# Batch 0 of a cosformer attention by halves of its heads, ahead of a two-GEMM MLP

## The chip, the cores and the metric

The kernel runs on one core of a Trainium2 chip. The metric is the device time of one execution in microseconds: 300.6 us is the median of three runs of the kernel before the change (300.25 to 301.1). The profile is of one further execution, whose span on the core is 298.9 us.

## The reference

A linear attention with position-weighted features, followed by an MLP with a squared ReLU. There are 8 batches, 8 heads, 576 positions and a head width of 64; the model width is 512 and the hidden width 2048.

```python
def phi(x, c, s):                        # c = cos, s = sin of pi/2 * pos / 576
    r = np.maximum(x, 0.0)
    return np.concatenate([r * c, r * s], axis=-1)
q_p, k_p = phi(q, cos_w, sin_w), phi(k, cos_w, sin_w)
kv  = np.einsum('bhsf,bhsd->bhfd', k_p, v)
z   = np.sum(k_p, axis=2)
num = np.einsum('bhsf,bhfd->bhsd', q_p, kv)
den = np.einsum('bhsf,bhf->bhs', q_p, z)[..., None] + 1e-06
x   = (num / den)                        # heads side by side: 4608 rows of 512
h   = np.maximum(x @ w_in, 0.0)          # w_in 512 x 2048
out = (h * h) @ w_out                    # w_out 2048 x 512
```

## The kernel before

Each batch is cut into four pieces of 128 positions (`j` = 0 to 3, "main") and a tail of 64 positions (`j` = 4 = `J`), whose two halves of the heads lie above each other on the partitions. The kernel's work is a list of "column slots": `gemm1` slots multiply x (transposed) by a part of w_in, `gemm2` slots multiply the squared hidden values by w_out. The attention of later batches is put between these slots. Batch 0's attention has no slots to lie between and stands ahead of them.

The loads of batch 0 go out on SyncE's queue, one issue for the main part of each of k, v, q, and two for each tail:

```python
    def load(src, nm, b, eng):
        main = inp.tile([P, H, J, D], F32, name=nm, tag=nm, bufs=2)
        tail = inp.tile([P, HH, D], F32, name=nm + "t", tag=nm + "t", bufs=2)
        eng.dma_start(out=main[:, :, :, :],
                      in_=src[b, :, 0:MAIN, :].rearrange("h (p j) d -> p h j d", j=J))
        for g in range(2):
            eng.dma_start(out=tail[g * TAIL : (g + 1) * TAIL, :, :],
                          in_=src[b, g * HH : (g + 1) * HH, MAIN:S, :].rearrange("h p d -> p h d"))
```

What stands ahead of the first slot, in the order in which each engine gets it:

```python
        load_batch(0, nc.sync, "kvq")
        constants()
        for j in range(NS):
            att_k(0, j)                  # cosine features on VectorE, sine features on ScalarE
            if j < J:
                warm(j)                  # two matmuls of 512 columns whose result nobody reads
        att_v(0, J - 1, nc.gpsimd, H - 1, H)   # one head of v cast by GpSimd
        att_v(0, 0, nc.vector)
        att_v(0, 1, nc.scalar)
        att_v(0, 2, nc.vector)
        att_v(0, 3, nc.vector, 0, H - 1)
        att_v(0, J, nc.vector)
        for i in range(4):
            load_w1(i, 4)                # GpSimd's queue, behind its cast
        load_batch(1, nc.gpsimd, "qkv")
        for i in range(4):
            load_w2(i, 4)
        load_batch(2, nc.gpsimd, "qkv")
        att_kv(0, 0)                     # kv and z in one: v has a column of ones
        att_kv(0, 1)                     # ends with a copy of kv from PSUM (kvz) on ScalarE
        for j in range(J):
            warm(j)
        att_feat(0, 0)                   # features of q, pieces 0 and 1
        att_feat(0, 1)
        for j in range(2):
            att_qT_pe(0, j, True)        # transposes of 8 heads on TensorE
        for j in range(2):
            att_qT_copy(0, j, True)      # PSUM to SBUF, half on VectorE, half on ScalarE
            att_num(0, j, True)
        for j in range(2):
            att_div(0, j)                # den, reciprocal, product on VectorE: x
        att_feat(0, 2, "s")
        att_feat(0, 3, "s")
        for j in range(2):
            fill(4 - j)                  # matmuls whose result nobody reads
            att_x_pe(0, j, True)         # x transposed on TensorE, copied by ScalarE
        att_feat(0, 2, "c")
        att_feat(0, 3, "c")
        att_qT_pe(0, 2)
        att_qT_copy(0, 2, True)
        for s in range(len(slots)):
            run(s)
```

`load_w1(i, 4)` and `load_w2(i, 4)` each bring a quarter of a weight matrix, converted from fp32 to bf16 by the DMA. `gemm1` slot `s` of a batch needs quarter `s % 4` of w1. Slots 0 to 7 are `gemm1` of batch 0; slots 8 to 15 are `gemm2` of batch 0, and slot 8 needs the first quarter of w2:

```python
        step = P if (b, s) == (0, 0) else w        # slot 0 in two parts of 128 columns
        for c in range(0, w, step):
            for i in range(nh):
                hb = h0 + i
                for kb in range(KB):
                    ...                            # matmul of w1sb[:, kb, hb] with xT[:, kb, c:c+step]
```

The two remaining pieces of batch 0 are finished between the first slots:

```python
    at(0, att_qT_pe, 0, 3)
    at(0, att_num, 0, 2)
    at(0, att_qT_copy, 0, 3, True)
    at(0, att_div, 0, 2)
    at(1, att_x_pe, 0, 2, True)
    at(1, att_d, 0, 3)
    at(2, att_x_pe, 0, 3, True)
```

Of the kernel before, what the change touches and what calls it, by code (L numbers as in the profile page):

```python
# [15 lines left out]
FP = 512  # L16
# [3 lines left out]
def kernel(  # L20
# [40 lines left out]
    def load(src, nm, b, eng):  # L61
        main = inp.tile([P, H, J, D], F32, name=nm, tag=nm, bufs=2)
        tail = inp.tile([P, HH, D], F32, name=nm + "t", tag=nm + "t", bufs=2)
        eng.dma_start(
            out=main[:, :, :, :],
            in_=src[b, :, 0:MAIN, :].rearrange("h (p j) d -> p h j d", j=J),
        )
        for g in range(2):
            eng.dma_start(  # L69
                out=tail[g * TAIL : (g + 1) * TAIL, :, :],  # L70
                in_=src[b, g * HH : (g + 1) * HH, MAIN:S, :].rearrange("h p d -> p h d"),
            )
        kqv[nm, b] = (main, tail)

    def load_batch(b, eng, order):
        for nm in order:
            load({"k": k, "v": v, "q": q}[nm], nm, b, eng)
# [6 lines left out]
    ident = const.tile([P, P], BF16, name="ident")  # L84
    cos_col = const.tile([P, J + 1], F32, name="cos_col")
    sin_col = const.tile([P, J + 1], F32, name="sin_col")

    def constants():
        sidx = const.tile([P, J + 1], F32, name="sidx")
        for p0, p1, c, n, base, mult in [  # L90
            (0, P, 0, J, 0, J),
            (0, TAIL, J, 1, MAIN, 1),
            (TAIL, P, J, 1, MAIN, 1),
        ]:
            nc.gpsimd.iota(
                sidx[p0:p1, c : c + n],
                pattern=[[1, n]],
                base=base,
                channel_multiplier=mult,
                allow_small_or_imprecise_dtypes=True,  # L100
            )
        bias_pi2 = const.tile([P, 1], F32, name="bias_pi2")
        nc.vector.memset(bias_pi2, math.pi / 2.0)
        theta_scale = (math.pi / 2.0) / S
        nc.scalar.activation(cos_col, sidx, ACTF.Sin, bias=bias_pi2[:], scale=-theta_scale)
        nc.scalar.activation(sin_col, sidx, ACTF.Sin, bias=0.0, scale=theta_scale)
        make_identity(nc, ident)

# [52 lines left out]
    def xT_of(b, i):  # L161
        return cached(xts, (b, i), [P, KB, 2 * P], "xT", 4)
# [5 lines left out]
    def feat_cos(dst, src, j):  # L168
        nc.vector.tensor_scalar(  # L169
            out=dst[:, :, 0:D],  # L170
            in0=src,
            scalar1=0.0,
            scalar2=cos_col[:, j : j + 1],
            op0=ALU.max,
            op1=ALU.mult,
        )

    def feat_sin(dst, src, j):
        nc.scalar.activation(  # L179
            out=dst[:, :, D:F], in_=src, func=ACTF.Relu, scale=sin_col[:, j : j + 1]  # L180
        )

    def att_k(b, j):
        for f in (feat_cos, feat_sin):
            f(kp_of(b, j), piece("k", b, j), j)

    def att_v(b, j, eng, h0=0, h1=H):
        copy = eng.copy if eng is nc.scalar else eng.tensor_copy
        vx, vxt = vexts[b % 2]
        if j == J:  # L190
            copy(out=vxt[:, :, 0:D], in_=piece("v", b, j))
        else:
            copy(out=vx[:, j, h0:h1, 0:D], in_=piece("v", b, j)[:, h0:h1, :])  # L193

    def warm(j):

        wm = ps_h.tile([P, 2, FP], F32, name="wm", tag="hps", bufs=2)
        for i in range(2):
            nc.tensor.matmul(  # L199
                out=wm[:, i, :],  # L200
                lhsT=ident[:, :],
                rhs=kp_of(0, j)[:, i * HH : (i + 1) * HH, :],
                start=True,
                stop=True,
            )

    def fill(n):

        wm = ps_a.tile([P, 2, FP], F32, name="wm", tag="pa", bufs=1)
        for i in range(n):  # L210
            nc.tensor.matmul(  # L211
                out=wm[:, i % 2, :],
                lhsT=ident[:, :],
                rhs=kp_of(0, 0)[:, 0:HH, :],
                start=True,
                stop=True,
            )

    def att_kv(b, part):
        vx, vxt = vexts[b % 2]  # L220
        if part == 0:
            kvzs[b] = att.tile([P, H, E1], BF16, name="kvz", tag="kvz", bufs=2)
            kzs[b] = ps_a.tile([P, 2, FP], F32, name="kz", tag="pa", bufs=1)
        kz = kzs[b]
# [4 lines left out]
        for j in (0, 1) if part == 0 else range(2, NS):  # L229
            for hh in range(HH):  # L230
                for half in range(2):
# [12 lines left out]
                    )  # L244
        if part == 1:
            nc.scalar.copy(
                out=kvzs[b].rearrange("p (a h) e -> p a (h e)", a=2),
                in_=kz[:, :, 0 : HH * E1],
            )

    def att_feat(b, j, parts="cs"):
        for c in parts:
            f = feat_cos if c == "c" else feat_sin
            f(qp_of(b, j), piece("q", b, j), j)
# [15 lines left out]
    def att_qT_pe(b, j, apart=False):  # L270

        nh = H if j < J else HH
        tq = ps_y.tile([P, H, P], BF16, name="tq", tag="yps", bufs=2)
        tqs[b, j] = [tq[:, 0:HH, :]]
        if apart:
            hi = ps_h.tile([P, HH, P], BF16, name="tqh", tag="hps", bufs=2)
            tqs[b, j].append(hi)
        elif nh == H:
            tqs[b, j].append(tq[:, HH:H, :])
        for h in range(nh):  # L280
            nc.tensor.transpose(  # L281
                tqs[b, j][h // HH][:, h % HH, :], qp_of(b, j)[:, h, :], ident[:, :]
            )

    def att_qT_copy(b, j, both=False):
        qpTs[b, j] = []
        for i, tq in enumerate(tqs[b, j]):
            t = att.tile([P, HH, P], BF16, name=f"qpTp{i}", tag=f"qpTp{i}", bufs=5)
            copy = nc.scalar.copy if both and i else nc.vector.tensor_copy
            copy(out=t[:, :, :], in_=tq[:, :, :])  # L290
            qpTs[b, j].append(t)

    def att_num(b, j, early=False):
        qpT, kvz = qpTs[b, j], kvzs[b]
        if early:
            num = ps_h.tile([P, 2, FP], F32, name="num", tag="hps", bufs=2)
        else:
            num = ps_a.tile([P, 2, FP], F32, name="num", tag="pa", bufs=1)
        for hh in range(HH):
            for half in range(2):  # L300
# [9 lines left out]
        nums[b, j] = num  # L310

    def att_div(b, j):
        n = 2 if j < J else 1
        n4 = nums[b, j][:, 0:n, 0 : HH * E1].rearrange("p b (h e) -> p b h e", e=E1)
# [7 lines left out]
            out=x_of(b, j).rearrange("p (b k) (l d) -> p b k l d", b=n, l=2),  # L322
# [18 lines left out]
    def att_x_pe(b, j, in_y=False):  # L341
        nk = KB if j < J else 2
# [4 lines left out]
        for kb in range(nk):  # L347
            nc.tensor.transpose(tx[:, kb, :], x_of(b, j)[:, kb, :], ident[:, :])  # L348
        if j < J:
            dst = xT_of(b, j // 2)[:, :, j % 2 * P : (j % 2 + 1) * P]  # L350
        else:
            dst = xT_tails(b // 2)[:, b % 2].rearrange("p k g c -> p k (g c)")
        nc.scalar.copy(out=dst, in_=tx[:, 0:nk, :])
# [5 lines left out]
    def gemm1(b, s):  # L359
# [9 lines left out]
        step = P if (b, s) == (0, 0) else w  # L369
# [125 lines left out]


    at(0, att_qT_pe, 0, 3)
    at(0, att_num, 0, 2)
    at(0, att_qT_copy, 0, 3, True)
    at(0, att_div, 0, 2)  # L500
    at(1, att_x_pe, 0, 2, True)
    at(1, att_d, 0, 3)
    at(2, att_x_pe, 0, 3, True)
# [48 lines left out]
    with tc.manual_schedule():  # L552
        load_batch(0, nc.sync, "kvq")
        constants()
        for j in range(NS):
            att_k(0, j)
            if j < J:
                warm(j)
        att_v(0, J - 1, nc.gpsimd, H - 1, H)
        att_v(0, 0, nc.vector)  # L560
        att_v(0, 1, nc.scalar)
        att_v(0, 2, nc.vector)
        att_v(0, 3, nc.vector, 0, H - 1)
        att_v(0, J, nc.vector)
        for i in range(4):
            load_w1(i, 4)
        load_batch(1, nc.gpsimd, "qkv")
        for i in range(4):
            load_w2(i, 4)
        load_batch(2, nc.gpsimd, "qkv")  # L570
        att_kv(0, 0)
        att_kv(0, 1)
        for j in range(J):
            warm(j)
        att_feat(0, 0)
        att_feat(0, 1)
        for j in range(2):
            att_qT_pe(0, j, True)
        for j in range(2):
            att_qT_copy(0, j, True)  # L580
            att_num(0, j, True)
        for j in range(2):
            att_div(0, j)
        att_feat(0, 2, "s")
        att_feat(0, 3, "s")
        for j in range(2):
            fill(4 - j)
            att_x_pe(0, j, True)
        att_feat(0, 2, "c")
        att_feat(0, 3, "c")  # L590
        att_qT_pe(0, 2)
        att_qT_copy(0, 2, True)
# [31 lines left out]
```

## Time and profile before

| | before |
|---|---|
| time, median of 3 runs | 300.6 us |
| span of the profiled execution | 298.9 us |
| TensorE matmul busy | 285.7 us (96%) |
| ScalarE busy | 154.0 us (52%) |
| VectorE busy | 135.5 us (45%) |
| GpSimd busy | 48.0 us (16%) |
| moved by DMA | 52.98 MB, mean 177 GB/s |

In the lines of the profile, PE is TensorE's matmuls, PEld its weight loads, DVE VectorE, ACT ScalarE, POOL GpSimd, SP SyncE. L380 is line 380 of the kernel. `out<-in` names the tiles that an instruction writes and reads, and a group in the timeline gives its start in us from the span's start and its length, with the idle time before it and what ended that in square brackets. Transposes on TensorE count as matmuls. A "landing" is the moment at which a DMA's completion reaches the semaphore that others wait on. GB/s counts the bytes written, so w1 and w2, which are read as fp32 and written as bf16, show half of what they read. In a table by stages, each row has the stage, its length, busy time and count of PE, PEld, DVE, ACT and POOL, the granted clock, the DMA share and GB/s.

### The profile page before, as it was taken

To read this page: it belongs to the slowest core of one execution; us is meant where nothing else is said; L and a number is where in the kernel's file an instruction comes from. 1 tells how busy PE (TensorE), PEld (TensorE's weight loads), DVE (VectorE), ACT (ScalarE), POOL (GpSimd) and SP (SyncE) were. 2 spreads that over 40 slices of the span, in tenths; PEclk is the share of its full clock that TensorE was granted. 3 is DMA by queue.
4 is the path that set the end of the run, shared out by engine and by line. 5 is a ranking of instruction groups with operands and counts; after the bars stand their busy time and mean duration, and the time that the engine had idled before them with its cause. 6 is when DMAs were issued, how large, how long until landed. Compare 5 with 4: busy or idle time off the path is not lost.

```text
span 298.9 us, 6372 instructions
## 1 busy us (share of the span) xinstructions
PE 285.7 (96%) x2636; PEld 200.6 (67%) x2659; DVE 135.5 (45%) x330; ACT 154.0 (52%) x215; POOL 48.0 (16%) x79
## 2 busy tenths in 40 slices
PE   0899999999999999999999999999999999999995
PEld 0469855889556984589654884589754894589544
DVE  1455664465648386228730287227740273024100
ACT  3466753666838564655554555555563552255311
POOL 1554304751121002000021001100021000100000
PEclk9999999999999999999999999999999999999999
DMA  7999993999648996896779925798669013100021
GB/s 216 293 206 352 276 243 102 352 362 209 171 99 148 242 269 157 239 278 181 122 170 221 334 47 124 235 271 227 114 178 212 35 37 79 72 36 2 33 75 70
DMA packets 77069, 52.98 MB, mean 177 GB/s; under 512 B 52240, under 2 KB 71952, under 8 KB 77040
## 3 DMA queue, kind: packets, MB, share of 16 engines
q1 hardware_dynamic: 67120, 29.50, 42.7%
q0 software_dynamic: 9776, 22.94, 26.8%
q8 instruction: 21, 0.34, 0.4%
q10 hardware_dynamic: 144, 0.13, 0.1%
q14 instruction: 8, 0.07, 0.1%
HBM read 36.70 MB, written 9.44 MB: 154 GB/s over the span
## 4 chain that ended last, share of the span: by engine, by line
PE 93%; DMA 3%; ACT 1%; issue 1%; DVE 1%; SPq 1%; ACTq 0%
PE hps L380 42%; PE yps L415 39%; PE kz L238 4%; PE num L307 3%; DMA v<-in_v_dram 3%; PE yh L415 2%; PE tq L281 1%; PE wm L199 1%; PE tx L348 1%; PE wm L211 1%; SPq L69 0%; ACT qpTp L290 0%; ACT rt L388 0%; DVE qpTp L290 0%; DVE gTt L395 0%
## 5 line engine op out<-in xcount | busy, mean ns | idle before, releaser
L380 PEld LDWEIGHTS <-w1sb 128*128 128x128 bf16 x1296 | 113.0, 98 | 12.3
L380 PE MATMUL hps<-xT,w1sb 128*128 128x256 bf16 (+1 forms) x1040 | 117.8, 271 | 0.0
L415 PE MATMUL yps<-w2sb,gT 128*128 128x512 bf16 (+1 forms) x476 | 108.1, 372 | 1.4 <-DVE qpTp L290 0.2
L388 ACT ACTIVATE rt<-hps 128x1024 bf16<-128x1024 f32 x72 | 73.7, 1024 | 57.8 <-DVE gT L395 32.6
L415 PEld LDWEIGHTS <-gT 128*128 128x128 bf16 x528 | 49.5, 98 | 53.0 <-DVE qpTp L290 0.7
L395 DVE TENSOR_TENSOR gT<-rt 128x1024 bf16<-128x1024 bf16 x64 | 44.0, 688 | 84.5 <-ACT rt L388 84.5
L411 POOL DMA_DIRECT2D out_dram<-ysb x34 | 20.7, 610 | 176.5 <-ACT ysb L401 174.3
L401 ACT COPY ysb<-yps 128x512 f32<-128x512 f32 (+1 forms) x35 | 20.0, 575 | 56.1 <-PE yps L415 56.0
L179 ACT ACTIVATE qp<-q,sin_col 128x512 bf16<-128x512 f32 x32 | 21.9, 718 | 5.0 <-DMA q<-in_q_dram 5.0
L179 ACT ACTIVATE kp<-k,sin_col 128x512 bf16<-128x512 f32 x32 | 21.1, 713 | 3.2 <-DMA k<-in_k_dram 3.2
L321 DVE TENSOR_TENSOR x<-num,rden 128x512 bf16<-128x512 f32 x32 | 22.1, 691 | 1.1
L169 DVE TENSOR_SCALAR qp<-q,cos_col 128x512 bf16<-128x512 f32 x32 | 14.4, 489 | 11.7 <-DMA q<-in_q_dram 11.7
L169 DVE TENSOR_SCALAR kp<-k,cos_col 128x512 bf16<-128x512 f32 x32 | 15.1, 481 | 5.0 <-DMA k<-in_k_dram 5.0
L317 DVE TENSOR_SCALAR den<-num 128x8 f32<-128x8 f32 (+1 forms) x40 | 6.6, 165 | 22.3 <-PE num L307 22.1
L380 PE MATMUL hps<-xTt,w1sb 128*128 128x128 bf16 x256 | 15.3, 219 | 0.0
L415 PE MATMUL yps<-w2sb,gTt 128*128 128x512 bf16 x64 | 14.5, 379 | 0.0
L193 DVE CAST vext<-v 128x512 bf16<-128x512 f32 (+1 forms) x31 | 13.0, 425 | 2.7 <-DMA v<-in_v_dram 2.7
L238 PEld LDWEIGHTS <-kp 128*128 128x128 bf16 x256 | 10.3, 102 | 4.0 <-issue 1.6
L199 PE MATMUL wm<-kp,ident 128*128 128x512 bf16 x15 | 6.0, 553 | 7.2 <-ACT kp L179 7.0
L307 PEld LDWEIGHTS <-qpT 128*128 128x128 bf16 (+1 forms) x240 | 10.3, 100 | 3.3 <-issue 1.7
L307 PE MATMUL num<-kvz,qpT 128*128 128x65 bf16 (+1 forms) x240 | 11.7, 194 | 0.0
L238 PE MATMUL kz<-vext,kp 128*128 128x65 bf16 x256 | 10.7, 199 | 0.8 <-DVE vext L193 0.8
(56 smaller groups left out, 130.2 us busy)
## 6 DMA issues: line engine op xcount, KB each, us to landing
out_dram<-ysb POOLq DMA_DIRECT2D x28, 256.0 KB, 3.5
k<-in_k_dram SPq DMA_DIRECT2D x5, 1024.0 KB, 6.1
v<-in_v_dram SPq DMA_DIRECT2D x5, 1024.0 KB, 8.1
q<-in_q_dram SPq DMA_DIRECT2D x5, 1024.0 KB, 6.0
q<-in_q_dram POOLq DMA_DIRECT2D x3, 1024.0 KB, 13.5
k<-in_k_dram POOLq DMA_DIRECT2D x3, 1024.0 KB, 10.3
v<-in_v_dram POOLq DMA_DIRECT2D x3, 1024.0 KB, 9.8
w1sb<-in_moe_w_in_dram POOLq DMA_DIRECT2D x4, 512.0 KB, 8.2
```

The source lines that it names most:

```text
L169: nc.vector.tensor_scalar(out=dst[:, :, 0:D], in0=src, scalar1=0.0, scalar2=cos_col[:, j : j + 1], op0=ALU.max, op1=ALU.mult,)
L179: nc.scalar.activation(out=dst[:, :, D:F], in_=src, func=ACTF.Relu, scale=sin_col[:, j : j + 1])
L193: copy(out=vx[:, j, h0:h1, 0:D], in_=piece("v", b, j)[:, h0:h1, :])
L238: nc.tensor.matmul(out=kz[:, half, hh * E1 : (hh + 1) * E1], lhsT=lhsT, rhs=rhs, start=(j == 0 and hh == 0), stop=(j == J and hh == HH - 1),)
L307: nc.tensor.matmul(out=out, lhsT=lhsT, rhs=kvz[:, half * HH + hh, :], start=True, stop=True)
L321: nc.vector.tensor_tensor(out=x_of(b, j).rearrange("p (b k) (l d) -> p b k l d", b=n, l=2), in0=n4[:, :, :, 0:D].rearrange("p b (k l) d -> ...
L380: nc.tensor.matmul(out=out, lhsT=w1sb[:, kb, hb * P : (hb + 1) * P], rhs=rhs, start=(kb == 0), stop=(kb == KB - 1),)
L388: nc.scalar.activation(out=rt[:, :, :], in_=hps[:, :, :], func=ACTF.Relu)
L395: nc.vector.tensor_tensor(out=dst, in0=rt[:, :, :], in1=rt[:, :, :], op=ALU.mult)
L401: nc.scalar.copy(out=ysb[:, c0:c1], in_=acc)
L411: eng.dma_start(out=dst, in_=ysb[p0 : p0 + n, c0:c1])
L415: nc.tensor.matmul(out=acc, lhsT=lhsT, rhs=w2sb[:, hb, c0:c1], start=(hb == 0), stop=(hb == HB - 1))
```

## The change

Batch 0 is loaded by halves of its heads: k, v, q of heads 0 to 3, then k, v, q of heads 4 to 7. Features, kv, num and x of the first half are worked through while the second half is on its way, so that after the last bytes only half of the heads is left to do. The first and the fifth column slot run in two parts of 128 columns, so that the first part can begin when the first piece of x is there. The warm-up matmuls read a tile of zeros and start at once instead of waiting for k. Query pieces 2 and 3 are transposed after slot 0. GpSimd still casts one head of v ahead of the weight loads; it is head 7, part of the second half.

The diff, cut to its core (helpers that only gained a `half` argument are left out, as marked):

```diff
-    def load(src, nm, b, eng):
-        main = inp.tile([P, H, J, D], F32, name=nm, tag=nm, bufs=2)
-        tail = inp.tile([P, HH, D], F32, name=nm + "t", tag=nm + "t", bufs=2)
+    def load(src, nm, b, eng, half=None):
+        ...                              # the two tiles, made once
+        main, tail = kqv[nm, b]
+        h0, h1 = (0, H) if half is None else (half * HH, (half + 1) * HH)
         eng.dma_start(
-            out=main[:, :, :, :],
-            in_=src[b, :, 0:MAIN, :].rearrange("h (p j) d -> p h j d", j=J),
-        )
-        for g in range(2):
+            out=main[:, h0:h1, :, :],
+            in_=src[b, h0:h1, 0:MAIN, :].rearrange("h (p j) d -> p h j d", j=J),
+        )
+        for g in range(2) if half is None else (half,):
 ... (features, v casts, kv, transposes, num, division, x: each for one half of the heads)
-    def warm(j):
+    def warm(n):
         wm = ps_h.tile([P, 2, FP], F32, name="wm", tag="hps", bufs=2)
-        for i in range(2):
+        for i in range(n):
             nc.tensor.matmul(
-                out=wm[:, i, :],
-                lhsT=ident[:, :],
-                rhs=kp_of(0, j)[:, i * HH : (i + 1) * HH, :],
-                start=True,
-                stop=True,
+                out=wm[:, i % 2, :], lhsT=ident[:, :], rhs=zeros[:, :], start=True, stop=True
             )
 ...
-        step = P if (b, s) == (0, 0) else w
+        step = P if b == 0 and s % 4 == 0 else w
 ...
-    at(0, att_qT_pe, 0, 3)
-    at(0, att_num, 0, 2)
-    at(0, att_qT_copy, 0, 3, True)
-    at(0, att_div, 0, 2)
-    at(1, att_x_pe, 0, 2, True)
-    at(1, att_d, 0, 3)
-    at(2, att_x_pe, 0, 3, True)
+    both = [nc.vector, nc.scalar]
+    for j in (2, 3):
+        at(0, att_qT_pe, 0, j)
+        at(0, att_qT_copy, 0, j, both)
+    at(1, att_d, 0, 2)
+    at(2, att_x_pe, 0, 2, True)
+    at(2, att_d, 0, 3)
+    at(3, att_x_pe, 0, 3, True)
 ...
-        load_batch(0, nc.sync, "kvq")
+        for half in range(2):
+            load_batch(0, nc.sync, "kvq", half)
         constants()
-        (the rest of the order ahead of slot 0, shown above)
+        warm(14)
+        for half in range(2):
+            for j in range(NS):
+                att_k(0, j, half)
+            if half == 1:
+                for j in range(2):
+                    fill(3)
+                    att_x_pe(0, j, True, 0)
+
+                att_v(0, 3, nc.gpsimd, None, (H - 1, H))
+                for i in range(4):
+                    load_w1(i, 4)
+                load_batch(1, nc.gpsimd, "qkv")
+                for i in range(4):
+                    load_w2(i, 4)
+                load_batch(2, nc.gpsimd, "qkv")
+            att_v(0, 0, nc.vector, half)
+            att_v(0, 1, nc.scalar, half)
+            att_v(0, 2, nc.vector, half)
+            if half == 0:
+                att_v(0, 3, nc.scalar, half)
+            else:
+                att_v(0, 3, nc.vector, None, (HH, H - 1))
+            att_v(0, J, nc.vector, half)
+            kv_mms(0, range(NS), (half,))
+            fill(4)
+            att_feat(0, 0, "cs", half)
+            att_feat(0, 1, "c", half)
+            kvz_copy(0, half, half + 1)
+            att_feat(0, 1, "s", half)
+            for j in range(2):
+                att_qT_pe(0, j, half)
+                att_qT_copy(0, j, [both[j]] * 2, half)
+            fill(2)
+            for j in range(2):
+                att_num(0, j, True, (half,))
+            for j in range(2):
+                att_div(0, j, half, half + 1)
+        att_feat(0, 2, "s")
         for j in range(2):
+            if j == 0:
+                fill(3)
+            att_x_pe(0, j, True, 1)
+        att_feat(0, 3, "s")
         att_feat(0, 2, "c")
         att_feat(0, 3, "c")
-        att_qT_pe(0, 2)
-        att_qT_copy(0, 2, True)
         for s in range(len(slots)):
             run(s)
```

## The prediction

> **What bounds the kernel now.** I read the page first: the span, the busy shares, the chain that ended last.
>
> ```profile
> span 298.9 us, 6372 instructions
> PE 285.7 (96%) x2636; PEld 200.6 (67%) x2659; DVE 135.5 (45%) x330; ACT 154.0 (52%) x215; POOL 48.0 (16%) x79
> ...
> PE hps L380 42%; PE yps L415 39%; PE kz L238 4%; PE num L307 3%; DMA v<-in_v_dram 3%; PE yh L415 2%; PE tq L281 1%; PE wm L199 1%; PE tx L348 1%; PE wm L211 1%; SPq L69 0%; ACT qpTp L290 0%; ACT rt L388 0%; DVE qpTp L290 0%; DVE gTt L395 0%
> ```
>
> TensorE holds 93% of the chain. Only a front part, before the first column slot, isn't a row of GEMM matmuls. So I next read the chain in order of time for the first 40 us (start, length, what).
>
> ```profile
> 2.71 8.13 DMA v<-in_v_dram
> ...
> 16.66 1.08 ACT qpTp L290 x2
> ...
> 21.05 1.79 PE hps L380 x32
> ...
> 37.49 0.46 PE tq L281 x8
> 37.95 0.02 issue
> 37.97 0.77 DVE qpTp L290 x2
> 38.74 0.05 issue
> 38.78 0.39 PE yps L415
> ```
>
> The first 10.8 us are loads of k and v, then batch 0's attention runs as one serial chain, and the first column slot begins at 20.9 (its first matmul; the chain books the end of the transposes to 21.05). From there the chain is TensorE without a gap, except for one small stop at 38. Seen like this, whatever pulls slot 0 forward shortens the whole kernel. Before believing that I asked what else the slots need: the weights. The timeline of GpSimd shows when their loads are issued.
>
> ```profile
> 10.89 0.49 POOL L193 CAST vext<-v 128x64 bf16<-128x64 f32 x1 [9.02 <-DMA v<-in_v_dram]
> 11.32 3.17 POOL L115 DMA_DIRECT2D w1sb<-in_moe_w_in_dram  x4
> ...
> 28.22 0.62 POOL L69 DMA_DIRECT2D vt<-in_v_dram  x1 [2.29 <-DMA q<-in_q_dram]
> 28.83 1.52 POOL L122 DMA_DIRECT2D w2sb<-in_moe_w_out_dram  x2
> ```
>
> GpSimd casts one head of v only after v has landed, and issues w1 behind it in its own order. After that its queue carries w1, batch 1, w2, batch 2. The DMA view cut to the first w1 issue, and cut to the first w2 issue, gives the time to landing (last column).
>
> ```profile
> w1sb<-in_moe_w_in_dram POOLq DMA_DIRECT2D x1, 512.0 KB, 5.5
> ...
> w2sb<-in_moe_w_out_dram POOLq DMA_DIRECT2D x1, 512.0 KB, 8.9
> ```
>
> So w1's first quarter is there at 11.32 + 5.5 = 16.8, 4.1 us before slot 0 uses it. The fourth is issued at 13.73 and takes 11.3, so it lands at 25.0; slot 3 starts at about 27.5, a slack of 2.5. And w2's first quarter lands at 28.83 + 8.9 = 37.7. Who uses it is in the timeline:
>
> ```profile
> 37.33 0.61 PE L281 MATMUL tq<-ident,qp 128*128 128x128 bf16 x8
> ...
> 37.80 0.39 PE L415 MATMUL yh<-w2sb,gT 128*128 128x512 bf16 x1
> ```
>
> Slot 8, the first of the second GEMM, starts at 37.80, and the weights it needs landed at 37.7. The slack is under 0.1 us. This is the number on which my prediction rests: the first 37.8 us have two limits of the same length, the TensorE chain and the DMA stream up to w2's first quarter. The chain shows only the first.
>
> **Is that stream full?** The DMA share is at or above 1 in nearly every stage from 5 to 35 us, with one hole, around the end of q:
>
> ```profile
> 12.40:12.80 0.40, 0.40 (x12) 0.40 (x10) 0.00 (x0) 0.00 (x0) 0.40 (x1) 1.00 0.72 197
> 12.80:13.20 0.40, 0.40 (x11) 0.31 (x9) 0.00 (x0) 0.00 (x0) 0.40 (x2) 1.00 0.53 101
> 13.20:13.60 0.40, 0.40 (x10) 0.31 (x10) 0.00 (x0) 0.00 (x0) 0.40 (x1) 1.00 0.60 98
> ```
>
> The last two columns are DMA share and GB/s. SyncE's loads run dry at about 13.2; the w1 stream, issued from 11.32, is at its full 205 GB/s of written bf16 only from about 14. From there to w2's landing it never pauses.
>
> **What the Trainium skill says.** "DMA: Bandwidth & Descriptors", section "Issuing engines are not separate DMA queues": DMAs started by different engines run on the same 16 DMA engines and interleave. The trace agrees: SyncE's queue has a 108% share alone from 11 to 12 us, GpSimd's 123% from 14 to 15, and between them they share. The same page, section "Anatomy of one DMA — SWDGE (gpsimd) path", gives a DMA from GpSimd a fixed 2.0 us or so besides its bytes. Here the first quarter of w1 takes 5.5, and successive quarters land about 2.7 apart, which leaves 2.8 fixed; I use the trace. "TensorE: Matmul & The Clock Gate", section "What's actually happening": a cold TensorE runs at half clock until about 3.4 us of activity, and an idle window of that length makes it cold again. The trace agrees with the warm-up: the 512-column warm matmuls start 0.43 apart at 7 us and 0.22 apart from 15.1 on.
>
> **The change part by part.**
> First, loads by halves. Bytes and packet sizes stay; twelve issues replace nine at 0.5 to 0.7 us each, so issuing still runs ahead of the bytes. In the new order (k, v, q of heads 0-3, then k, v, q of heads 4-7) the items end at sixths of the same 3.54 MB. In the kernel before k was there at 6.1 (0.73 + 5.4), v at 10.84 and q at 13.9. By bytes on that curve, k of the first half lands at about 4.7, v 6.3, q 8.7; of the second half k 10.5, v 12.5, q 14.1. So first-half data is far earlier, the last of q no earlier, and the **last of v comes 1.7 us later**, since half of q now lies ahead of it.
>
> Second, the path from the last q to slot 0. Half-width features: the 256-element tails took 0.35 on VectorE and 0.49 on ScalarE, against 0.48 and 0.71 at 512. From q at 14.1: sine features 0.5, transposes and their latency 0.4, copy 0.4 (ScalarE's for the second piece ends about 1 us later, behind the copy of kvz and its feature), num 0.3; then two divisions one after the other of about 0.85 (0.17 + 0.20 + some 0.45 for half of the 0.69), a transpose 0.4. That puts slot 0 at 18.3 to 18.5, against 20.89: **2.5 us gained** on this path.
>
> Third, work moved behind slot 0. The transposes of query piece 2 (0.6) leave the path before slot 0 and come after it, and slot 4 in two parts costs 32 matmuls in 1.95 instead of 16 in 1.75, so 0.2. Of the 2.5 some 1.7 would remain at slot 5.
>
> Fourth, GpSimd's cast now takes head 7, which comes with the second half. Its release moves from 10.84 to about 12.5, and with it the first w1 issue from 11.32 to 12.8 or 13.0. SyncE's loads still end at about 13.2, so the hole in the DMA stream grows by the whole delay; nothing makes it up, as the stream was full behind it. I take 1.5 us. Then w1 lands at 18.3, ..., 26.5, and w2's first quarter at 37.73 + 1.5 = 39.2.
>
> **The sum.** TensorE: slot 0 at 18.4, slot 3 held by w1 until 26.5 and done by 28.5 (29.5 before), slot 4 with 0.4 of added work, so ready for slot 8 at about 37.2. It must wait there until 39.2 or 39.3: 1.5 later than 37.80. Given back is the stop in slot 8 (third matmul at 38.24, next at 38.78 instead of 38.46: 0.3), as the copies it waited for are done during the wait. Net +1.2 us; everything after slot 8 is the same TensorE row and just moves. 300.6 + 1.2 = 301.8; I say 301.7.
>
> **Rivals.** (a) The gain survives: if w1 isn't late, 1.7 us come off at slot 5, but w2 still lands at 37.7, so slot 8 can't start earlier. Only the 0.3 of the stop would be won: 300.3. A real gain of 1.5 to 2 needs w2 earlier too, for which I see nothing in the diff: 299. (b) TensorE's idle stretch of about 2 us ahead of slot 8, or one between the halves at 11 to 13, makes it cold: cold slots 0 and 1 cost up to 3 us, most of it hidden by w2's lateness; a cold slot 8 costs 1.5 to 2: 303. The idle stretches are under the 3.4 us, so I give this a tenth. (c) v of the second half lands early, say at 11.7, because its small tails overlap: delay 0.8, time 301.1.
>
> **Range and chances.** The delay of w1 between 0.5 and 2.3 us gives 300.6 to 302.6; with (a) below and (b) above it I say 300.4 to 302.7. A change of 2% is 6 us, and no step here is worth that: same 0.98, the rest split.
>
> **What would show it.** Right: the first w1 issue at 12.5 to 13.2; slot 0's first matmul at 18 to 19; w2's first quarter landing at 38.8 to 39.7 and slot 8 starting with it after TensorE idled 1 to 2.5 us; from there the same spacing. Wrong: w1 issued at 11.5 or earlier, slot 8 starting before 37.5, or TensorE late for slot 8 by itself, with w2 waiting.

## The result, and the profile after

The changed kernel takes 302.84 us (median of 4 runs, 302.63 to 303.92) against 300.65 us for the kernel before on the same chip. The ratio is 1.008, with a 95% interval of 1.0052 to 1.0107: 2.2 us slower. The prediction was 301.7 with a range up to 302.7, so the direction was right and the size was half of what came. The profile is of the slowest of the four executions (303.92); the other three took 302.63 to 302.86, so the distances read from it below are about 1 us longer than in a typical one.

The page of the changed kernel, span, busy shares and the granted clock in tenths:

```profile
span 302.1 us, 6482 instructions
PE 290.9 (96%) x2687; PEld 203.5 (67%) x2687; DVE 139.0 (46%) x347; ACT 156.4 (52%) x227; POOL 47.4 (16%) x79
...
PEclk9969999999999999999999999999999999999999
```

Look at the third digit of the clock row: in the slice from 15.1 to 22.7 us TensorE had 0.6 of its speed on average. All 9s stood in that row before. The second thing to see is what is not there: from the fifth column slot on the activation of every slot of the first GEMM starts 2.96 us later in the changed kernel, to within 0.01 us, up to the last. So 2.96 of the 3.2 us between the two spans arise up to slot 4, and behind it the same work just moves, as the prediction said. The rest, 0.3 us, lies at the very end: from the landing of the last output to the end of the execution the changed kernel and each of its variants below take 1.22 to 1.23 us in their profiles, the kernel before and its variants 0.92 to 0.93. No part of the prediction has it, and its cause is open.

The table of stages of the changed kernel has the granted clock third from the right:

```profile
14.00:16.00 2.00, 0.53 (x12) 0.43 (x12) 1.94 (x6) 1.53 (x5) 2.00 (x4) 1.00 0.49 38
...
18.00:20.00 2.00, 1.55 (x13) 1.00 (x11) 0.42 (x1) 1.30 (x4) 2.00 (x4) 0.50 1.24 203
20.00:22.00 2.00, 1.62 (x13) 0.97 (x14) 1.83 (x8) 0.97 (x2) 0.55 (x2) 0.50 1.24 209
```

TensorE hardly works from 14 to 16 us (0.53), VectorE is full there (1.94), and from 16.8 to 23.7 the clock is at half. The DMA share from 14 to 16 is 0.49: the predicted hole, grown. Now the chain in order of time (start, length, what):

```profile
3.35 6.30 DMA q<-in_q_dram
...
13.27 1.28 DVE kp L192 x4
...
15.12 0.91 DVE vext L220 x3
...
16.06 0.53 DVE vextt L220
...
16.92 0.97 PE kz L234 x4
...
21.66 0.39 PE tx L377 x2
22.06 2.62 PE hps L409 x32
...
33.11 2.80 PE hps L409 x32
```

The chain no longer comes from the last loads. It comes from the *first* half's q, runs through the first half's divisions, then through VectorE's k features and v casts of the second half (13.27 to 16.59), then a row of filling matmuls at half clock (0.97), and slot 0 itself takes 2.6 instead of the 1.8 that the same 32 matmuls had in the chain before. The second half of k had landed at 11.4 and waited for VectorE; v had landed at 13.1 and q at 14.5.

The weights. GpSimd's timeline, and the DMA view cut to the first w2 issue:

```profile
13.13 0.24 POOL L220 CAST vext<-v 128x64 bf16<-128x64 f32 x1 [11.25 <-DMA v<-in_v_dram]
13.30 3.16 POOL L122 DMA_DIRECT2D w1sb<-in_moe_w_in_dram  x4
...
31.30 1.52 POOL L129 DMA_DIRECT2D w2sb<-in_moe_w_out_dram  x2
```

```profile
w2sb<-in_moe_w_out_dram POOLq DMA_DIRECT2D x1, 512.0 KB, 8.4
```

w1's first issue went from 11.32 to 13.30, and w2's first quarter lands at 31.30 + 8.4 = 39.7 instead of 37.7. Last, slot 8:

```profile
40.28 0.61 PE L306 MATMUL tq<-ident,qp 128*128 128x128 bf16 x8
...
40.73 0.59 PE L444 MATMUL yh<-w2sb,gT 128*128 128x512 bf16 x2
```

Slot 8 starts right behind the transposes, 1 us after w2 landed. In this execution TensorE itself was late, not the weights. Two explanations of the loss stand: **stream** (w2's first quarter, at the end of a DMA stream that started late, holds slot 8) and **chain** (VectorE's order and the half clock make TensorE late by itself). The runs had to tell whether it was one, the other, or both.

### The profile page after: what moved, and what is told of

The parts are those of the page before. It is cut to its first block, busy times and chain, and to the rows that moved or that the text cites. A ratio compares the mean times of both kernels' runs of the same rounds, so it can differ in the third digit from the quotient of the medians.

```text
span 302.1 us, 6482 instructions
## 1 busy us (share of the span) xinstructions
PE 290.9 (96%) x2687; PEld 203.5 (67%) x2687; DVE 139.0 (46%) x347; ACT 156.4 (52%) x227; POOL 47.4 (16%) x79
## 3 DMA queue, kind: packets, MB, share of 16 engines
q1 hardware_dynamic: 67168, 29.50, 40.7%
## 4 chain that ended last, share of the span: by engine, by line
PE 92%; DVE 2%; DMA 2%; ACT 1%; SPq 1%; issue 1%; ACTq 0%
PE hps L409 42%; PE yps L444 39%; PE num L335 3%; PE kz L264 3%; PE yh L444 2%; DMA q<-in_q_dram 2%; PE tq L306 1%; PE tx L377 1%; DVE x L350 1%; PE kz L234 1%; SPq L75 0%; ACT qp L201 0%; DVE kp L192 0%; SPq L70 0%; PE tqh L306 0%
## 5 line engine op out<-in xcount | busy, mean ns | idle before, releaser
L409 PEld LDWEIGHTS <-w1sb 128*128 128x128 bf16 x1312 | 114.2, 98 | 12.7 <-issue 0.6
L409 PE MATMUL hps<-xT,w1sb 128*128 128x256 bf16 (+1 forms) x1056 | 119.0, 271 | 0.5 <-ACT xT L382 0.5
L444 PE MATMUL yps<-w2sb,gT 128*128 128x512 bf16 (+1 forms) x496 | 110.6, 372 | 0.2 <-DVE qpTp L316 0.2
L417 ACT ACTIVATE rt<-hps 128x1024 bf16<-128x1024 f32 x72 | 73.7, 1024 | 58.9 <-DVE gT L424 32.8
L440 POOL DMA_DIRECT2D out_dram<-ysb x34 | 20.5, 605 | 176.2 <-ACT ysb L430 174.2
L201 ACT ACTIVATE qp<-q,sin_col 128x512 bf16<-128x512 f32 (+1 forms) x34 | 22.7, 695 | 7.7 <-DMA q<-in_q_dram 7.7
L350 DVE TENSOR_TENSOR x<-num,rden 128x512 bf16<-128x512 f32 (+1 forms) x34 | 22.4, 660 | 1.2
L201 ACT ACTIVATE kp<-k,sin_col 128x512 bf16<-128x512 f32 (+1 forms) x36 | 22.0, 667 | 1.6 <-DMA k<-in_k_dram 1.6
L192 DVE TENSOR_SCALAR qp<-q,cos_col 128x512 bf16<-128x512 f32 (+1 forms) x34 | 14.9, 478 | 11.9 <-DMA q<-in_q_dram 11.8
L192 DVE TENSOR_SCALAR kp<-k,cos_col 128x512 bf16<-128x512 f32 (+1 forms) x36 | 16.0, 458 | 3.1 <-DMA k<-in_k_dram 3.1
L444 PE MATMUL yps<-w2sb,gTt 128*128 128x512 bf16 x64 | 14.5, 379 | 0.0
L220 DVE CAST vext<-v 128x512 bf16<-128x512 f32 (+2 forms) x33 | 13.3, 410 | 2.1 <-DMA v<-in_v_dram 2.1
L444 PEld LDWEIGHTS <-gTt 128*128 128x128 bf16 x64 | 6.3, 98 | 7.5
```

Source lines behind the costliest of these rows:

```text
L192: nc.vector.tensor_scalar(out=dst[:, :, 0:D], in0=src, scalar1=0.0, scalar2=col_of(cos_col, j, half), op0=ALU.max, op1=ALU.mult,)
L201: nc.scalar.activation(out=dst[:, :, D:F], in_=src, func=ACTF.Relu, scale=col_of(sin_col, j, half))
L220: copy(out=dst, in_=src)
L350: nc.vector.tensor_tensor(out=x_of(b, j)[:, 2 * b0 : 2 * b1].rearrange("p (b k) (l d) -> p b k l d", b=n, l=2), in0=n4[:, :, :, 0:D].rearr ...
L409: nc.tensor.matmul(out=out, lhsT=w1sb[:, kb, hb * P : (hb + 1) * P], rhs=rhs, start=(kb == 0), stop=(kb == KB - 1),)
L417: nc.scalar.activation(out=rt[:, :, :], in_=hps[:, :, :], func=ACTF.Relu)
```

## The experiments

Each run is compared with the kernel before on the same chip (medians of 300.3 to 300.6 in these comparisons). The mean granted clock of TensorE was measured in every execution: in the profiled ones it is 0.998 or more where the clock held in the front part, and 0.994 or less where it fell there for 3.41 us or longer.

### Does a late w1 alone slow the kernel before?

```diff
-        att_v(0, J - 1, nc.gpsimd, H - 1, H)
+        scr = const.tile([P, D], BF16, name="scr")
+        nc.gpsimd.tensor_copy(out=scr, in_=piece("q", 0, 3)[:, H - 1, :])
...
-        att_v(0, 3, nc.vector, 0, H - 1)
+        att_v(0, 3, nc.vector, 0, H)
```

> The kernel before, with one thing changed: GpSimd's small cast waits for q instead of v (and VectorE casts the whole fourth piece of v), so w1's first issue moves from 11.3 to about 14.3. Theory 'stream' (w2's first quarter, at the end of one full DMA stream, holds slot 8): w2's first quarter lands at about 40.8 instead of 37.8, slot 8 starts there, time 303.2 to 303.6. Theory 'chain' (only TensorE's own row ahead of slot 8 counts): no change, 300.6 to 300.9.

Measured: 307.63 us, ratio 1.0224 (1.0184 to 1.0263). TensorE's slots 1 to 7 were up to 1.15 later, and then in the timeline:

```profile
42.47 1.03 PE L415 MATMUL yh<-w2sb,gT 128*128 128x512 bf16 x2 [3.39 <-DMA w2sb<-in_moe_w_out_dram]
```

TensorE stood 3.39 us and w2's DMA ended it. The stream theory holds in kind: w2's landing can hold the kernel before as well. But w1 was issued 3.2 later and w2 landed 4.7 later, more than either theory had, and after the wait slot 8 ran at half clock to 48.5, which fits the rest of the 7 us: 6.0 us at half clock lose some 3.0, an estimate from this trace.

### Releasing w1 early in the changed kernel

```diff
-                att_v(0, 3, nc.gpsimd, None, (H - 1, H))
+                scr = const.tile([P, D], BF16, name="scr")
+                nc.gpsimd.tensor_copy(out=scr, in_=piece("k", 0, 3)[:, H - 1, :])
...
-                att_v(0, 3, nc.vector, None, (HH, H - 1))
+                att_v(0, 3, nc.vector, None, (HH, H))
```

> The changed kernel, with GpSimd released by the second half of k (landed 11.4) instead of the second half of v (13.1); VectorE casts head 7 of v. w1's first issue at about 11.7. Theory 'stream': w2's first quarter lands at about 38.0, the time falls by 1.6 or so to 301.2. Theory 'chain' (slot 8 at 40.7 is set by batch 0's attention on VectorE and TensorE): w2 lands earlier but slot 8 stays, time 302.5 to 303. If GpSimd's issuing slows VectorE, VectorE's casts and features between 11.7 and 15 are the slow ones instead of those from 13.3 to 16.5.

Measured: 304.43 us, slower than the changed kernel. Nothing of the expectation came: w1's issue at 12.4, v at 14.2 and q at 16.0 (13.1 and 14.5 in the changed kernel), half clock from 15.7 to 26.0, and w2 at 40.2. The second half of k, which no w1 competed with, was late as well (12.2 instead of 11.4). That was the first sign of a disturbance in the experiment itself, found further down.

### Keeping TensorE busy in its gap

```diff
+            if half == 1:
+                fill(16)
             kv_mms(0, range(NS), (half,))
```

> The changed kernel with 16 more idle matmuls of 252 columns ahead of the second half's kv, in the gap from 13.6 to 15.5 where TensorE waits for VectorE. Theory 'cold' (the half clock from 16.8 to 23.7 costs the path): the granted clock stays full, slot 0 takes 1.95 instead of 2.82 and the fill matmuls 0.1 each, slot 8 comes 1.3 to 1.8 earlier but not before w2 lands at 39.7, time 301.8. Theory 'chain by VectorE' alone: within 0.3 of 302.8. Theory 'stream': the time was already at w2's landing, so no more than 0.3 to 0.5.

Measured: 302.74 us (302.21 to 303.14). The clock stayed full, slot 0 started at 19.6 instead of 21.8 and took 1.95, and the time did not move. This reading of the clock doesn't rest on the profiled executions alone: its mean is 0.999 to 1.0 in all four here, and 0.989 to 0.993 in all four of the changed kernel. The timeline shows what took the gain:

```profile
39.36 0.60 PE L444 MATMUL yh<-w2sb,gT 128*128 128x512 bf16 x2 [1.09 <-DMA w2sb<-in_moe_w_out_dram]
```

TensorE was ready at 38.3 and waited 1.09 for w2. With the clock mended the stream is the bound.

### VectorE's order

```diff
-                for j in range(2):
-                    fill(3)
-                    att_x_pe(0, j, True, 0)
...
             att_feat(0, 1, "s", half)
+            if half == 1:
+                att_div(0, 0, 0, 1)
             for j in range(2):
                 att_qT_pe(0, j, half)
                 att_qT_copy(0, j, [both[j]] * 2, half)
+            if half == 1:
+                att_div(0, 1, 0, 1)
...                                      (the division of half 1 behind its num as before, x transposed whole)
```

> The changed kernel with the first half's two divisions (and its transposes of x) moved behind the second half's features of q, so VectorE takes the second half's k and v as they land. Theory 'chain by VectorE': k features start at 11.4 instead of 13.3 and the second half's kv at about 14 instead of 15.5; slot 0 comes 1.0 to 1.5 earlier; slot 8 earlier by the same, until w2 holds it at 39.7; time 302.0. Theory 'cold': TensorE's gap changes its place, slot 0 stays slow, time 302.5. Theory 'stream': under 0.4.

Measured: 302.82 us. k features started at 11.4, the second half's kv at 13.6, slot 0 at 20.5, 1.3 earlier than in the changed kernel; TensorE then waited 1.07 for w2, which landed at 40.0.

```profile
11.40 1.14 DVE L192 TENSOR_SCALAR kp<-k,cos_col 128x256 bf16<-128x256 f32 x4 [0.76 <-DMA k<-in_k_dram]
...
40.08 0.60 PE L444 MATMUL yh<-w2sb,gT 128*128 128x512 bf16 x2 [1.07 <-DMA w2sb<-in_moe_w_out_dram]
```

The clock was at half in this run too (13.1 to 19.9), so a mended clock isn't what made slot 0 earlier: the 1.3 is VectorE's order, and mending it alone buys nothing.

### Moving w2's first quarter ahead

```diff
-                load_batch(1, nc.gpsimd, "qkv")
-                for i in range(4):
+                load_batch(1, nc.gpsimd, "q")
+                load_w2(0, 4)
+                load_batch(1, nc.gpsimd, "kv")
+                for i in range(1, 4):
                     load_w2(i, 4)
```

The same edit was put on four kernels: the kernel before with w1 late, the changed kernel, the changed kernel kept warm, and the kernel before.

> The kernel before with w1 late as in the earlier run (that took 307.6), and w2's first quarter loaded ahead of batch 1's k and v. Theory 'stream': slot 8 no longer waits for w2 (which lands at about 35), TensorE does not go cold there; what stays is the wait of slots 1 to 3 for w1 (1.15 in the earlier trace): time 301.3 to 301.8. Theory 'chain': the earlier loss had another cause and most of it stays: over 305.

Measured: 304.36 us, 3.3 less than without the edit. Slot 8 no longer waited, but slot 10 waited 1.7 for the *second* quarter of w2 (44.6): I had overlooked that moving one quarter leaves the next where it was.

> The changed kernel with only w2's first quarter moved ahead of batch 1's k and v. In the profiled execution of the changed kernel slot 8 came at 40.7 by itself while w2 was there at 39.7, in the others perhaps not. Theory 'stream' (most executions wait for w2): 1 us less, about 301.8. Theory 'chain plus cold TensorE': TensorE is as late by itself, time within 0.4 of 302.8.

Measured: 303.01 us, ratio 1.0081 (1.0059 to 1.0103): no gain. w2 was there at 32.8, and slot 8 came at 40.05 behind its own transposes, with the clock at half from 16.8 to 23.6. With the stream mended, the chain is the bound.

```profile
39.60 0.61 PE L306 MATMUL tq<-ident,qp 128*128 128x128 bf16 x8
40.05 0.38 PE L444 MATMUL yh<-w2sb,gT 128*128 128x512 bf16 x1
```

> The changed kernel kept warm in the gap, and w2's first quarter moved ahead. Kept warm alone it took 302.7 and waited 1.1 for w2. Both theories together (stream and cold): slot 8 at 38.2 to 38.5, time 301.2 to 301.7, with 0.5 of it from slots 3 and 4 (w1's last quarter and the copy of x). Theory 'chain by VectorE' alone: 302.5.

Measured: 301.83 us, ratio 1.0047 (1.0033 to 1.0061). Either edit alone gave nothing (302.74, 303.01), the two together gave 1.0. That is the answer to the main question: the changed kernel has **two limits of nearly equal length**, a chain at half clock and a late weight stream.

> Control: the kernel before with w2's first quarter moved ahead of batch 1's k and v. TensorE reached slot 8 at 37.8 by itself, so an earlier w2 alone should bring nothing: 300.3, within 0.3. If it gains 0.5 or more, most executions of the kernel before waited for w2 too.

Measured: 299.78 us, ratio 0.9984 (0.9971 to 0.9997). A small gain of 0.5, more than the control was to show. It would fit that some executions of the kernel before wait for w2 as well; no trace here shows one that does.

### The rest of the changed kernel's loss

Pieces 2 and 3 and the fifth slot put back, on top of the version that is warm and has w2 ahead:

```diff
-        step = P if b == 0 and s % 4 == 0 else w
+        step = P if (b, s) == (0, 0) else w
...                                      (the plan of pieces 2 and 3 as in the kernel before)
```

> The changed kernel kept warm and with w2's first quarter ahead (301.8), and with query pieces 2 and 3 and the one-part fifth slot put back as in the kernel before. There the trace lost 1.4 between slot 0 and slot 5 against the kernel before. If the moved pieces are that loss, slot 0 comes 0.6 later, slots 1 to 4 keep the old distances, slot 8 is 0.6 to 0.9 earlier: 301.0 to 301.3. If w1's landings (27.2 for the last quarter) hold slot 3 instead, 301.6 to 301.9.

Measured: 301.99 us. This median stands between two groups. The four executions whose clock held (0.998 to 1.0) took 301.1 to 301.4, as expected if the moved pieces are the loss, and some 0.5 less than the nine such executions of the version before it (median 301.8). The four in which the clock fell (0.993 and 0.994) took 302.6 to 303.2. The profiled execution, one of the first group, had slots 0 to 7 all 0.17 behind the kernel before, so the 1.4 between slot 0 and slot 5 was gone, but slot 0 had paid 0.95 for it (21.06 instead of 20.11). w1's last quarter landed at 27.4, some 0.3 ahead of slot 3: its lateness now left slot 0 little to win.

With the first half's divisions deferred (the edit above) and the four filling matmuls of the second half left out as well:

```diff
             if half == 1:
-                fill(16)
+                fill(12)
             kv_mms(0, range(NS), (half,))
-            fill(4)
+            if half == 0:
+                fill(4)
```

> As the one before it, and also with the first half's divisions behind the second half's features of q, and without the four filling matmuls between the second half's kv and its transposes. Theory 'chain by VectorE': slot 0 another 0.6 to 1.0 earlier. Theory 'stream': slots 1 to 3 then wait for w1 (last quarter at about 27), so the time does not follow: within 0.4 of the run before it, and a wait for w1 stands in the trace.

Measured: 301.29 us. The 0.7 less goes with the clock, not with VectorE's order: in the 13 of 20 executions whose clock held the median is 301.3, as in such executions of the run before it, and the other seven took 301.5 at the median instead of 303.0. Slot 0 came at 19.7, 1.4 earlier, and the time didn't follow; the list of TensorE's waits (us in total, times, longest) shows the stream:

```profile
PE yh L444 <- DMA w2sb<-in_moe_w_out_dram: 0.8, 1, 0.8
PE hps L409 <- DMA w1sb<-in_moe_w_in_dram: 0.7, 3, 0.4
```

Now the early warm-up, one part of the change, alone on the kernel before, without and with w2 ahead:

```diff
         constants()
+        warm0(14)                       # 14 matmuls on zeros, as in the changed kernel
...
-        for j in range(J):
+        for j in range(2):
             warm(j)
         att_feat(0, 0)
```

> The kernel before with one part of the change alone: 14 warm-up matmuls on zeros at the start; four of its eight warm-up matmuls ahead of the transposes of q left out. The transposes start at 14.8 instead of 16.0, slot 0 at about 19.9. Theory 'two equal limits': slot 8 still waits for w2 at 37.8, time 300.1 to 300.5, and the trace shows TensorE waiting there for w2's DMA about 1 us. Theory 'chain' only: 299.4.

Measured: 300.59 us, ratio 0.9997 (0.9984 to 1.0011): no gain. In the profiled execution the transposes started at 15.2, part of the front ran at half clock after all, and TensorE reached slot 8 at about w2's landing (37.6). The 1 us of waiting that the expectation had wasn't there to be seen.

> The same with w2's first quarter ahead of batch 1's k and v. Theory 'two equal limits': with both limits moved the time follows, 298.8 to 299.2, the only version here well under the kernel before. Theory 'chain' only: the same as without the move of w2.

Measured: 299.94 us, ratio 0.9973 (0.9963 to 0.9984). It beats both kernels, by 0.7 us against the kernel before, less than expected. That the early warm-up has a share in it isn't shown: w2 moved alone gave 0.9984 (0.9971 to 0.9997), and the intervals overlap. Slot 8 started at 35.7 in the profiled execution, but this was the fastest of 18 (298.6), and its loads had landed about 0.9 early.

### Is it the start of w1?

The edit of "Releasing w1 early" again, first on the version kept warm, then on the one with all the other edits.

> The changed kernel kept warm (302.7) and with GpSimd released by the second half of k. Released so without the warm matmuls it took 304.4, with TensorE at half clock for 10 us and the second half of v and q 1.2 to 1.4 later. Theory 'the delayed start of w1 is what the stream lost': w2's first quarter at 38.0 to 38.5, slot 8 there, 301.3. Theory 'the loads only share': what w1 gains v and q lose, slot 0 comes about 1 later, slot 8 by TensorE's chain at 39.3 or more, 302.5 or more.

Measured: 302.96 us. w1 was issued at 11.9, and yet w2 landed at 40.2, later than in the changed kernel.

> The version with all of the other changes (301.3, with waits of 0.7 for w1 and 0.8 for w2's second quarter in its trace), and GpSimd released by the second half of k. Theory 'start of w1': both waits go, 300.0 to 300.4. Theory 'the loads only share': the waits go, slot 0 comes 1 later, 301.0 to 301.6.

Measured: 301.84 us, again no gain (ratio 1.0044, 1.0019 to 1.0069, against 1.0021, 1.0011 to 1.0031, without the early w1). By the expectations as written, sharing would have won. But in the runs with a moved start of w1 the loads' 4 KB packets took 196 to 210 ns on average over the first 40 us, against 169 to 179 in all the others, and some loads were late before w1 joined. These runs have one more thing in common: the scratch tile of 128 bytes a partition for GpSimd's copy. It stands in the pool of constants and moves all tiles behind it by 128 bytes.

> The changed kernel with nothing but an extra, unused tile of 128 bytes a partition in the pool of constants. Theory 'address': the 4 KB packets of the batch loads take 195 to 208 ns instead of 177, w2's first quarter lands at 40.3 to 41, time 303.3 to 304.3. If the tile has no effect: 302.8, packets at 177.

```diff
         nc.vector.memset(zeros, 0.0)
+        pad = const.tile([P, D], BF16, name="pad")
+        nc.vector.memset(pad, 0.0)
```

Measured: 305.33 us, ratio 1.0162 (1.0125 to 1.02). A tile that nobody reads costs 2.5 us. Over the first 40 us the 4 KB packets took 200 ns on average, against 178 in the changed kernel. The DMA view of a stretch in which batch 1's loads run alone, first of the changed kernel (30.5 to 33.5 us), then of this one (32.6 to 36):

```profile
DMA packets 312, 1.09 MB, mean 365 GB/s; under 512 B 48, under 2 KB 48, under 8 KB 311
...
q0 software_dynamic: 311, 1.08, 101.1%
```

```profile
DMA packets 313, 1.10 MB, mean 323 GB/s; under 512 B 48, under 2 KB 48, under 8 KB 312
...
q0 software_dynamic: 312, 1.08, 101.9%
```

The same packets at the same share of the engines took 3.4 us instead of 3.0: each packet is 14% longer (1.019 x 16 x 3.4 / 312 = 0.178 us against 1.011 x 16 x 3.0 / 311 = 0.156). So the three main runs with a moved w1 were repeated with a scratch tile of 1024 bytes:

```diff
-scr = const.tile([P, D], BF16, name="scr")
+scr = const.tile([P, FP], BF16, name="scr")
```

> The kernel before with w1 late again, but GpSimd's scratch tile is 1024 bytes a partition instead of 128, so that the tiles behind it keep their place modulo 1024. In the first form the 4 KB packets of the loads took 202 ns instead of 174, and w2 came 4.7 later for a w1 issue 3.2 later. Theory 'the scratch tile moved the other tiles to addresses that the DMA serves slowly': packets at 174 again, w2's first quarter 3.0 to 3.3 later (40.8 to 41.1), slot 8 with it, TensorE not cold, time 303.2 to 303.8. Theory 'the w1 start alone made the stream slow': 4.7 later again, 305.7 to 307.6.

Measured: 303.58 us, ratio 1.0101 (1.0068 to 1.0134). w1 at 14.2, w2 at 41.1, slot 8 with it:

```profile
41.13 0.66 PE L415 MATMUL yh<-w2sb,gT 128*128 128x512 bf16 x2 [2.19 <-DMA w2sb<-in_moe_w_out_dram]
```

As expected, 2.9 later issued and 3.3 later landed; only the clock fell again after the wait in this execution. Three of the eight, with a mean clock of 0.994, took 305.2 to 305.5; the five whose clock held took 301.9 to 303.7.

> The changed kernel kept warm and with w1 released by the second half of k, with the scratch tile of 1024 bytes. Theory 'address': packets at 177, w1's first issue at 11.4 to 11.7, w2's first quarter at 37.9 to 38.4, slot 8 at 38.5 to 39 (TensorE's own chain), time 301.3 to 302.0 instead of 303.0. Theory 'the loads only share': 302.5 or more.

Measured: 301.54 us, 1.2 less than kept warm alone. w1 at 11.6, w2 at 38.0, and slot 8 (38.7) waits for nothing but TensorE.

> The version with all the changes and w1 early, with the scratch tile of 1024 bytes. Theory 'start of w1': waits for w1 and w2 gone, 300.0 to 300.5, level with the kernel before. Theory 'the loads only share': 301.0 to 301.6.

Measured: 300.57 us, ratio 1.0007 (0.9989 to 1.0024): level with the kernel before. With these edits nothing of the 2.2 us is left, and by the median nothing gained either: q lands at 15.0 in this run, 1 us later than in the kernel before, and slot 0 starts when it did there. The clock is still a loss here: it fell in 13 of 20 executions, which took 301.9 at the median, and the seven in which it held took 300.2.

## Why the prediction was wrong

- **The second limit.** Right. That w2's landing and TensorE reach slot 8 of the kernel before together was read from the profile, and the runs with a late w1 show TensorE standing there for w2's DMA.
- **GpSimd's release with the second half of v.** Right in kind, mis-sized: v at 13.1 instead of 12.5, w1 at 13.30 instead of 12.8 to 13.0, the shift of w2's landing 1.9 (to 39.67 from 37.76) instead of 1.5. (The low end of the range, a delay of 0.5, is 300.8 by the sum given, not 300.6.)
- **The path from the last q to slot 0: this is the step that failed.** It was put at 4.2 us from q at 14.1, "That puts slot 0 at 18.3 to 18.5", a gain of 2.5. (The terms listed there add up to 3.7; what makes up the rest isn't said.) Slot 0 came at 21.8, 7.3 after q at 14.5. I had added up durations as if every engine stood free when the last bytes arrived. VectorE was then still at the second half's k and v until 16.6, because the first half's divisions stood ahead of them in its queue: 1.3 of slot 0's lateness, by the run that deferred them. The first half's loads, too, were later than the count by bytes had them: v at 8.0 instead of 6.3, q at 9.65 instead of 8.7. And TensorE ran at half clock. From the start of the second half's kv to slot 0 it took 6.4 us, kept warm 5.0, so the clock is at most 1.4 of the lateness, and slot 0 itself took 0.9 longer. Slot 0 was 2.2 earlier in the run kept warm, but 0.8 of that was there before the clock mattered, as its loads were earlier. The start of kv in the changed kernel, then kept warm:

```profile
15.47 0.90 PE L264 MATMUL kz<-vext,kp 128*128 128x65 bf16 x16 [1.86 <-DVE vext L220]
```

```profile
14.66 0.69 PE L264 MATMUL kz<-vext,kp 128*128 128x65 bf16 x16
```

- **"ready for slot 8 at about 37.2".** Failed with it: 40.7 in the profiled execution, and the prediction's own sign of being wrong, TensorE late for slot 8 with w2 waiting, was there. The run with w2 ahead shows that this alone gives the whole measured time (303.0).
- **The work moved behind slot 0.** Under-sized. 0.8 was added; in the trace the activation of slot 0 is 1.84 late and that of slot 4 2.96, so 1.1, and 0.9 of it comes at slot 4 alone (0.22 for a transpose, 0.2 for the two parts, 0.47 waiting for ScalarE's copy of x, which now stands behind slot 3's activation).
- **"Given back is the stop in slot 8", 0.3.** Not in the profiled execution: TensorE came late by its own chain and met the same stop (41.16, next 41.74). Where TensorE waited for w2 (kept warm) the stop was gone.
- **Rival (b), TensorE cold.** It got a tenth, on the argument that the idle stretches are under 3.4 us. The longest was 1.86 and the clock fell. This is the judgment to correct; what the clock followed instead stands in the last section.

The stream's term was short as well. Kept warm, where slot 8 waited for w2, the profiled execution was 1.5 longer than that of the kernel before (spans 300.4 and 298.9), against 1.2 predicted. It was the fastest of its four, and their median, 302.74, is 2.2 above the kernel before by the ratio. So either limit alone gives about the whole loss, and the prediction had only one of the two. Which of them ends last in an execution that was not profiled can't be told: they lie within about 1 us of each other, and mending one alone changed nothing.

## What to carry to other kernels

A chain of waits shows one limit. Before work is moved, list for each later consumer when its data land, and give the slack; where it is near zero a second limit is already there, and mending either alone can be worth nothing, as it was here (302.74 and 303.01 instead of 302.84). And when work is cut into halves, sum the engine's whole queue from the first half on, in its order: a half that comes first in the queue also stands ahead of the other.

## What the runs showed of the hardware

- **The clock falls without a long idle stretch.** The Trainium skill, "TensorE: Matmul & The Clock Gate", section "Why this matters for your kernels", asks for no idle gap over some 3 us between bursts of matmuls. Here the longest gap was 1.86 us, and the clock halved at 16.84 for 6.83 us, which is two windows of 3.41. The window before it, and the same stretch in the run kept warm (the second number is TensorE's busy time, the third from the right the clock):

```profile
13.43:16.84 3.41, 1.28 (x22) 1.02 (x21) 3.28 (x10) 2.07 (x6) 3.41 (x5) 1.00 0.63 82
```

```profile
13.43:16.84 3.41, 2.88 (x39) 2.31 (x37) 2.92 (x9) 1.95 (x6) 3.41 (x5) 1.00 0.74 105
```

TensorE was busy 1.28 of 3.41 us in the first and lost its clock; at 2.88 it kept it. The other traces narrow this down. Wherever the clock changes more than once in a trace, the changes are whole multiples of 3.41 us apart, so its windows can be laid out. Ten windows in the first 45 us have a fall of the clock right behind them. Their busy time, as the profile models it, is 0.86 to 1.99 us, and the longest gap in them is 0.69 to 2.56. This is the one with the shortest gap (all edits, w1 early, 1024-byte tile), with the window behind it:

```profile
14.54:17.95 3.41, 1.99 (x33) 1.40 (x32) 3.10 (x12) 2.38 (x5) 3.25 (x6) 1.00 1.24 206
17.95:21.37 3.42, 3.21 (x29) 2.75 (x29) 2.40 (x8) 1.69 (x3) 1.42 (x2) 0.50 1.25 208
```

Two windows with less than 1.99 kept the clock (1.79 and 1.97), as did all from 2.01 up, one of them with a gap of 1.41. So in these runs the fall goes with a busy time under about 2.0 of 3.41 us and not with the length of one gap; where exactly the limit lies isn't shown.

- **Where a tile lies in a partition changes the speed of the loads into it.** 128 bytes of padding made the packets 14% longer and the kernel 2.5 us slower. The Trainium skill, "DMA: Bandwidth & Descriptors", section "How a descriptor splits into AXI transactions", says that a transaction must start at a 256-byte boundary and that a descriptor which doesn't start there fetches bytes it doesn't use. Whether that is the reason here isn't shown: shifts of 128 and 1024 bytes were tried, and only the first was slow. An experiment that adds a small tile must keep the places of the others.
- VectorE's cast of v's tail (64 rows of 256) took 0.28 us in the first half and 0.53 in the second, while GpSimd was issuing w1; in the run kept warm it took 0.32 with GpSimd issuing too. What slowed it isn't settled.
